# Storing part of the second two batches by column halves: attention with a soft mixture of experts on one core

## The chip, the core and the metric

The kernel runs on one core of a Trainium2 chip. The metric is the device time of the program in microseconds (us); lower is better. The kernel before has a median of 191.47 us over three runs (191.35 to 192.05). A core has five engines with a queue each: TensorE (PE; PEld is its weight load), VectorE (DVE), ScalarE (ACT), GpSimd (POOL) and SyncE (SP). Transfers between the chip's memory and a core's own memory run on 16 DMA engines.

## What is computed

```python
# q, k, v: [8 batches, 8 heads, 576 tokens, 64]
scores = scale * q @ k.T                  # window: each token sees itself and the 63 before
attn   = softmax(where(mask, scores, -1e9)) @ v
x      = attn.transpose(0, 2, 1, 3).reshape(4608, 512)

logits = x @ phi                          # [4608, 32]: 8 experts x 4 slots
d      = softmax(logits, over the tokens)
slot_input = (d.T @ x).reshape(8, 4, 512)
slot_out[e] = relu(slot_input[e] @ w1[e]) @ w2[e]      # w1: 512x1024, w2: 1024x512
c      = softmax(logits, over the slots)
out    = c @ slot_out                     # [4608, 512] float32
```

The softmax over the tokens needs all 4608 of them, so the experts start only when attention is done, and no row of the output can be written before the experts are done with at least the columns of that row that are written.

## The kernel before

The order of every instruction on every engine is written out by hand. The first 150 us (a loop over 32 pairs of heads) do attention, the logits and the slot inputs. What the change touches is the tail behind that, from the experts on.

**Experts.** `first` is the first layer (half of its columns at a time), `turn_hidden` transposes the hidden rows, `second` and `second_last` are the second layer. The second layer is made in two column halves of 256 (`d` = 0 and 1, `DH` = 256), each summed over all experts in its own PSUM tile `ops[d]`; `second_last(d)` does the last two experts, whose w2 weights arrive last (tile `w2h` for the last expert, loaded by GpSimd's queue, one half of the columns after the other). ScalarE then casts a half into `osb` (L904 and L910).

**Tokens.** The output is given out by pairs of batches, k = 0 to 3, of 1152 tokens each. A pair is laid out as 128 partitions of nine tokens (`NE` = 9, index e), so that the nine rows of a partition lie next to each other in the output. For a batch b, `ct_all[:, b]` holds the slot weights c before their division, in an order in which they can't be multiplied yet. `spread(b)` brings them in order: five products with 0/1 weights into the PSUM tile `rp`, then one copy into `ct4[b // 2]`, on ScalarE or VectorE (L662). `sums(k)` makes the nine row sums of a pair with nine one-column products into `rp` and takes their reciprocals on VectorE (L675, into `rcs`). There is one `rp` buffer: whoever writes it waits for whoever read it last.

**Giving out.** `give(k, e0, ne, c0, nc_)` makes tokens e0 to e0 + ne - 1 of all 128 partitions of pair k, columns c0 to c0 + nc_: one product for each token into a PSUM tile `cp` (four buffers, a bank each: two tokens of a column half, or one whole token), then for each token an eviction that multiplies by the reciprocal, on ScalarE (L899) or VectorE (L897) in turn, bank by bank (`turn`), into one of seven SBUF buffers, and a store from SyncE's queue (L901). A store of column halves writes pieces of 1 KB; one of whole rows writes ne rows that lie next to each other, 6 KB for three tokens. A store that reuses a buffer waits for the store seven before it.

The tail's order before: `second(0, .)`, `second_last(0)`, the first column half of pair 0 in stores of 2, 2 and 5 tokens, `second(1, .)`, `second_last(1)`, the second column half of pair 0 in stores of 4 and 5 tokens with `spread(2)` and `spread(3)` behind them, `sums(1)`, then pairs 1 to 3 as whole rows, three tokens at a time, with the spreads and sums of the next pair in between. That is 14 stores.

Of the kernel before, what the change touches and what calls it, by code (L numbers as in the profile page):

```python
# [9 lines left out]
FP32 = mybir.dt.float32  # L10
# [8 lines left out]
def kernel(  # L19
# [126 lines left out]
    DH = D // 2  # L146
# [11 lines left out]
    def w2_at(e, d, fc):  # L158
        return w2_t[e][d][fc] if e == last else w2_t[e][fc][:, DH * d:DH * d + DH]
# [331 lines left out]
    def cb_exp(b):  # L491
        ec = pw.tile([128, 6, 32], FP16, name="ec", tag="ec") if b < B - 1 else \
            lh[:, 6:8, :].rearrange("p i x -> p (i x)")[:, 0:192].rearrange("p (i s) -> p i s", s=32)
        nc.scalar.activation(ec[:, :, :], lgs.pop(b)[:, :, :], AF.Exp)
        cbs[b] = ec

    def cb_turn(b):
        nc.vector.transpose(ct_all[:, b, :], cbs.pop(b)[:, :, :].rearrange("p i s -> p (i s)"))
# [142 lines left out]
    NE = 2 * S // 128  # L641
# [12 lines left out]
    def spread(b, copy, rp=None):  # L654
        if rp is None:
            rp = psr.tile([128, 1024], FP32, name="rp", tag="rp")
        for t in range(5):
            w = 128 if t < 4 else 64
            nc.tensor.matmul(rp[:, 128 * t:128 * t + w], ss4[:, min(t, 3), :],
                             ct_all[:, b, 128 * (t // 4):128 * (t // 4) + w], start=True, stop=True,  # L660
                             skip_group_check=True)
        copy(out=ct4[b // 2][:, :, 64 * (b % 2):64 * (b % 2) + 64],  # L662
             in_=rp[:, 0:S].rearrange("p (x e) -> p e x", e=NE))
# [7 lines left out]
    def sums(k):  # L671
        rp = psr.tile([128, 1024], FP32, name="rp", tag="rp")
        for e in range(NE):
            nc.tensor.matmul(rp[:, e:e + 1], ct4[k][:, e, :], one[:, :], start=True, stop=True, skip_group_check=True)
        nc.vector.reciprocal(rcs[:, k, :], rp[:, 0:NE])  # L675

    b, p = B - 1, NP - 1
# [118 lines left out]
    psr = ctx.enter_context(tc.tile_pool(name="psr", bufs=1, space=bass.MemoryType.PSUM))  # L796
# [4 lines left out]
    def bank(name):  # L801
        t = psh.tile([128, 512], FP32, name=name, tag="ph")
        return t, t[:, :].bitcast(FP16)
# [23 lines left out]
    def turn_hidden(g):  # L827
        for i, copy in enumerate((nc.scalar.copy, nc.vector.tensor_copy)):
            _, th = bank("th")
            for c in range(4):  # L830
                nc.tensor.transpose(th[:, 128 * c:128 * c + 128], hs_[:, g, i, c, :], ident_h[:, :])
            copy(out=hT[g][:, 4 * i:4 * i + 4, :].rearrange("p c x -> p (c x)"), in_=th[:, 0:512])

    def second(d, g, js=range(4)):
        for fc in range(NFC):
            for j in js:
                nc.tensor.matmul(ops[d][32 * j:32 * j + 32, 0:DH], hT[g][:, fc, 32 * j:32 * j + 32],
                                 w2_at(4 * g + j, d, fc), start=(g == 0 and fc == 0), stop=False,
                                 skip_group_check=True)


    def second_last(d):
        for j in (2, 3):
            for fc in range(NFC):
                i = fc % 4
                nc.tensor.matmul(ops[d][32 * i:32 * i + 32, 0:DH], hT[1][:, fc, 32 * j:32 * j + 32],
                                 w2_at(4 + j, d, fc), start=False, stop=(j == 3 and fc >= 4), skip_group_check=True)

    act, dve = nc.scalar.copy, nc.vector.tensor_copy
# [15 lines left out]
    first(1, 1)  # L865
    second(0, 0)
    turn_hidden(1)
    cb_exp(b - 1)
    cb_turn(b - 2)
    second(0, 1, (0, 1))  # L870
# [9 lines left out]
    turn, piece = 0, 0  # L880

    def give(k, e0, ne, c0, nc_):
        nonlocal turn, piece
        ov = out[2 * S * k:2 * S * k + 2 * S, :].rearrange("(p e) d -> p e d", e=NE)
        ob = obs[piece % NRES][:, 0:ne * nc_].rearrange("p (e d) -> p e d", d=nc_)
        piece += 1
        n1 = 512 // nc_
        for i0 in range(0, ne, n1):
            n_ = min(n1, ne - i0)
            cp = pst.tile([128, n1, nc_], FP32, name="cp", tag="cp")  # L890
            for i in range(n_):
                nc.tensor.matmul(cp[:, i, :], ct4[k][:, e0 + i0 + i, :], osb[:, c0:c0 + nc_],  # L892
                                 start=True, stop=True, skip_group_check=True)
            for i in range(n_):
                rc = rcs[:, k, e0 + i0 + i:e0 + i0 + i + 1]
                if turn % 2:
                    nc.vector.tensor_scalar(out=ob[:, i0 + i, :], in0=cp[:, i, :], scalar1=rc, scalar2=None, op0=ALU.mult)  # L897
                else:
                    nc.scalar.activation(ob[:, i0 + i, :], cp[:, i, :], AF.Copy, scale=rc)  # L899
            turn += 1  # L900
        nc.sync.dma_start(out=ov[:, e0:e0 + ne, c0:c0 + nc_], in_=ob)  # L901

    second_last(0)
    act(out=osb[:, 0:DH], in_=ops[0][:, 0:DH])  # L904
    for e0, ne in ((0, 2), (2, 2), (4, 5)):
        give(0, e0, ne, 0, DH)
    second(1, 0)
    second(1, 1, (0, 1))
    second_last(1)
    act(out=osb[:, DH:D], in_=ops[1][:, 0:DH])  # L910
    for e0, ne in ((0, 4), (4, 5)):
        give(0, e0, ne, DH, DH)
        spread(2 + e0 // 4, (act, dve)[turn % 2])
    sums(1)
    for k in range(1, B // 2):
        for e0 in range(0, NE, 3):
            give(k, e0, 3, 0, D)
            if k < 3:
                if e0 < 6:
                    spread(2 * k + 2 + e0 // 3, (act, dve)[turn % 2])  # L920
                else:
                    sums(k + 1)
# [1 line left out]
_INS = ['q', 'k', 'v', 'moe_phi', 'moe_w1', 'moe_w2']  # L924
_OUTS = [((4608, 512), 'float32')]
# [25 lines left out]
```

## Time and profile before

| | |
|---|---|
| median of three runs | 191.47 us |
| the profiled execution | 191.22 us |
| its span, first to last instruction | 189.4 us |
| TensorE / VectorE / ScalarE busy | 160.4 / 142.9 / 144.9 us |
| stores of the output: issues, bytes | 14, 9.44 MB |
| first / last store issued | 160.49 / about 179.4 us |

The whole-kernel shares of busy time say little about the tail, the last 30 us. It is read by time windows (a row has the window, its length, then busy us and the number of instructions of TensorE, its weight loads, VectorE, ScalarE and GpSimd, then the granted TensorE clock, the mean busy share of the 16 DMA engines and the GB/s moved), by the timeline (start, us, engine, line, operation, and in brackets the idle time ahead of it and who ended it), and by the issues and landings of the stores. The share of the DMA engines can read somewhat over 1, since packets overlap.

### The profile page before, as it was taken

Reading aid. Unit: us, or ns where it says so; the run is one execution under the profiler, and the core shown is the slowest. Engines: PE = TensorE matmul, PEld = TensorE weight load, DVE = VectorE, ACT = ScalarE, POOL = GpSimd, SP = SyncE. Lnnn points to the kernel's source line nnn. Section 1 sums busy time; section 2 is a strip of 40 time slices with the busy share of each in tenths; the row PEclk is TensorE's granted clock in tenths of the full one; section 3 lists DMA queues with packets and bytes.
Section 4 is the critical chain, followed back from the end, with each engine's and each line's share of the span. In section 5 each row is a group of like instructions: output and inputs, shape, how many; then the busy total and the mean of one; then the engine's idle time right before and its main releaser. Section 6 shows DMA issues by size and latency. Waiting matters only on the chain. (4 is left out here: it accounts for less than half of the span.)

```text
span 189.4 us, 7060 instructions
## 1 busy us (share of the span) xinstructions
PE 160.4 (85%) x3036; PEld 120.5 (64%) x3036; DVE 142.9 (75%) x352; ACT 144.9 (76%) x266; POOL 98.5 (52%) x123
## 2 busy tenths in 40 slices
PE   5787999999999999999999899999989897769500
PEld 1466878877777777777777787776774365633100
DVE  6798796897888889788878988888886555289800
ACT  6487879989889898988999898988588256379600
POOL 7857927273695554983984828727854160000000
PEclk9999999999999999999999999999999999999955
DMA  6999999999999999999999999999999999979996
GB/s 153 222 184 185 226 175 223 179 223 179 185 226 180 210 192 184 207 196 185 210 195 192 211 182 198 199 204 195 213 214 212 204 196 179 277 258 422 415 415 252
DMA packets 61630, 41.47 MB, mean 219 GB/s; under 512 B 38816, under 2 KB 57504, under 8 KB 60704
## 3 DMA queue, kind: packets, MB, share of 16 engines
q0 software_dynamic: 56560, 30.35, 116.1%
q1 hardware_dynamic: 5040, 10.68, 15.9%
q8 instruction: 23, 0.38, 0.7%
q14 instruction: 7, 0.06, 0.1%
HBM read 61.93 MB, written 9.44 MB: 377 GB/s over the span
## 5 line engine op out<-in xcount | busy, mean ns | idle before, releaser
L336 ACT ACTIVATE qb<-a_q 64x576 f16<-64x576 f16 x63 | 40.6, 645 | 5.5 <-PE a_q L316 4.0
L353 DVE TENSOR_REDUCE m<-a_m 128x8 f16<-128x1024 f32 x32 | 39.2, 1224 | 1.0
L381 ACT ACTIVATE pt<-a_s 128x1024 f16<-128x1024 f32 x32 | 32.8, 1024 | 6.6 <-PE a_s L375 5.4
L180 POOL COPY v<-v 64x1152 f16<-64x1152 f16 x16 | 18.3, 1142 | 32.8 <-DMA v<-in_v_dram 32.6
L415 DVE TENSOR_TENSOR x_b<-a_v,rc 128x640 f16<-128x640 f32 x31 | 25.6, 825 | 1.1
L349 PEld LDWEIGHTS <-qb 128*128 128x128 f16 x256 | 16.8, 98 | 7.8 <-ACT qb L336 0.4
L346 PE MATMUL a_m<-wm,ident_h 128*128 128x512 f16 x64 | 19.3, 384 | 0.9 <-DVE m L353 0.9
L375 PEld LDWEIGHTS <-lh 128*128 128x128 f16 x288 | 18.8, 98 | 1.9 <-issue 1.7
L173 POOL DMA_DIRECT2D v<-in_v_dram x16 | 19.8, 1235 | 0.0
L372 PEld LDWEIGHTS <-kT 128*128 128x128 f16 x288 | 18.6, 98 | 1.6 <-issue 1.4
L372 PE MATMUL a_s<-qb,kT 128*128 128x128 f16 x256 | 19.5, 219 | 0.0
L349 PE MATMUL a_m<-kT,qb 128*128 128x128 f16 x256 | 19.5, 219 | 0.0
L375 PE MATMUL a_s<-rt,lh 128*128 128x128 f16 x256 | 19.5, 219 | 0.0
L433 ACT COPY xt<-a_k 128x576 f16<-128x576 f16 x28 | 17.9, 640 | 2.0 <-PE a_k L429 0.7
L182 POOL COPY v<-v 64x1088 f16<-64x1088 f16 (+1 forms) x16 | 17.9, 1120 | 0.8
L405 PE MATMUL a_v<-v,pt 128*64 128x65 f16 x558 | 15.6, 196 | 2.1 <-DVE m L363 1.1
L897 DVE TENSOR_SCALAR w<-cp,rcs 128x512 f32<-128x512 f32 (+1 forms) x22 | 12.9, 635 | 5.7 <-PE cp L892 5.4
L367 DVE CAST rt<-a_v 9x128 f16<-9x128 f32 x30 | 8.7, 289 | 11.0 <-PE a_v L366 10.7
L327 ACT ACTIVATE kT<-a_k 128x576 f16<-128x576 f16 x24 | 15.7, 654 | 0.8 <-PE a_k L316 0.8
L405 PEld LDWEIGHTS <-pt 128*64 128x64 f16 x576 | 13.5, 110 | 4.3 <-DVE m L363 1.8
L79 POOL DMA_DIRECT2D ks<-in_k_dram x15 | 10.4, 696 | 10.9 <-PE a_s L375 3.0
L316 PE MATMUL a_q<-ident_h,qs 96*64 96x96 f16 x384 | 14.7, 206 | 1.6 <-DVE a_q L225 1.3
(182 smaller groups left out, 332.6 us busy)
## 6 DMA issues: line engine op xcount, KB each, us to landing
w<-in_moe_w_dram POOLq DMA_DIRECT2D x13, 1024.0 KB, 16.8
out_dram<-w SPq DMA_DIRECT2D x9, 768.0 KB, 6.2
v<-in_v_dram POOLq DMA_DIRECT2D x16, 288.0 KB, 12.4
ks<-in_k_dram POOLq DMA_DIRECT2D x15, 288.0 KB, 15.2
qs<-in_q_dram POOLq DMA_DIRECT2D x15, 288.0 KB, 12.5
out_dram<-w SPq DMA_DIRECT2D x2, 640.0 KB, 4.4
w1h<-in_moe_w_dram POOLq DMA_DIRECT2D x4, 256.0 KB, 15.9
w<-in_moe_w_dram POOLq DMA_DIRECT2D x4, 256.0 KB, 14.8
```

The source lines that it names most:

```text
L173: nc.gpsimd.dma_start(out=v1s[b % 2][:, c, 0:Dh], in_=v[b].rearrange("h s d -> (h s) d").rearrange("(c p) d -> p c d", p=128)[:, c, :])
L180: nc.gpsimd.tensor_copy(out=v2[64:128, c0:c1, 0:Dh], in_=v1[0:64, c0:c1, 0:Dh])
L182: nc.gpsimd.tensor_copy(out=v2[0:64, c0:c1, 0:Dh], in_=v1[64:128, c0 - 1:c1 - 1, 0:Dh])
L336: nc.scalar.activation(qbs[p % NQ][h, :, hf, :], turned(a_qh)[h], AF.Copy, scale=QKS)
L346: nc.tensor.matmul(a_m[:, j, :], ident_h[:, :], wm[:, j:j + 4, :].rearrange("p c x -> p (c x)"), start=True, stop=False, skip_group_check= ...
L349: nc.tensor.matmul(a_m[:, i // 4, 128 * (i % 4):128 * (i % 4) + 128], qblock(p, i), kwindow(p, i), start=False, stop=True, skip_group_chec ...
L353: nc.vector.reduce_max(ms[p % 2][:, 64:72].rearrange("p (l c) -> p l c", l=2), a_m[:, :, :].rearrange("p l (c x) -> p l c x", x=128), axis ...
L372: nc.tensor.matmul(at(i), kwindow(p, i), qblock(p, i), start=(i % 4 == 0), stop=False, skip_group_check=True)
L375: nc.tensor.matmul(at(i), lh[:, i, :], rt[:, :], start=False, stop=True, skip_group_check=True)
L381: nc.scalar.activation(st_pt(p)[:, 0:8, :].rearrange("p i x -> p (i x)"), a_s[:, :, :], AF.Exp, scale=XS)
L405: nc.tensor.matmul(a_v[r0:r0 + 64, hf, 65 * (i // 2):65 * (i // 2) + 65], pt[:, i, 64 * hf:64 * hf + 64], rhs, start=True, stop=True, skip ...
L415: nc.vector.tensor_tensor(out=xbs[b][:, :, 128 * hp:128 * hp + 128].rearrange("p c (l d) -> p l c d", l=2), in0=avv[:, :, :, 0:64], in1=rc ...
```

## The change

`spread(2)` moves up to behind `turn_hidden(1)`. The products of `spread(3)` move ahead of the first `give` and its copy (VectorE) behind the second; for that `spread_product` makes the five products at once and keeps the copy for later in `late`. `sums(1)` moves ahead of `second_last(1)`. Three tokens of pair 1 are now stored by column halves: the first half ahead of `second_last(1)`, the second half behind pair 0's. The second column half of pair 0 is stored in pieces of 2, 3 and 4 tokens instead of 4 and 5. `spread(4)` and `spread(5)` come ahead of the whole rows of pair 1, `sums(2)` behind the first store of its whole rows, and pair 1 has two stores of whole rows instead of three. That is 16 stores.

```diff
     second(0, 0)
     turn_hidden(1)
+    spread(2, act)
     cb_exp(b - 1)
     cb_turn(b - 2)
     second(0, 1, (0, 1))
...
+    def spread_product(b):
+        rp = psr.tile([128, 1024], FP32, name="rp", tag="rp")
+        spread(b, lambda out, in_: late.append((out, in_)), rp)
+
     second_last(0)
     act(out=osb[:, 0:DH], in_=ops[0][:, 0:DH])
-    for e0, ne in ((0, 2), (2, 2), (4, 5)):
-        give(0, e0, ne, 0, DH)
+    late = []
+    spread_product(3)
+    give(0, 0, 2, 0, DH)
+    give(0, 2, 2, 0, DH)
+    dve(out=late[0][0], in_=late[0][1])
+    give(0, 4, 5, 0, DH)
     second(1, 0)
     second(1, 1, (0, 1))
+    sums(1)
+    give(1, 0, 3, 0, DH)
     second_last(1)
     act(out=osb[:, DH:D], in_=ops[1][:, 0:DH])
-    for e0, ne in ((0, 4), (4, 5)):
-        give(0, e0, ne, DH, DH)
-        spread(2 + e0 // 4, (act, dve)[turn % 2])
-    sums(1)
+    give(0, 0, 2, DH, DH)
+    give(0, 2, 3, DH, DH)
+    give(0, 5, 4, DH, DH)
+    spread(4, act)
+    give(1, 0, 3, DH, DH)
+    spread(5, dve)
     for k in range(1, B // 2):
-        for e0 in range(0, NE, 3):
+        for e0 in range(3 if k == 1 else 0, NE, 3):
             give(k, e0, 3, 0, D)
-            if k < 3:
+            if k == 1 and e0 == 3:
+                sums(2)
+            if k == 2:
                 if e0 < 6:
-                    spread(2 * k + 2 + e0 // 3, (act, dve)[turn % 2])
+                    spread(6 + e0 // 3, (act, dve)[turn % 2])
                 else:
-                    sums(k + 1)
+                    sums(3)
```

## The prediction

> **What bounds the kernel now.** First the chain that ended last, its last row and the span, and SyncE's own waits in the tail:
>
> ```profile
> span 189.4 us, 7060 instructions
> ...
> 178.82 0.58 ACTq L946
> ...
> SPq L946 <- DMA out_dram<-w: 7.5, 3, 3.8
> ```
>
> The chain stops at 179.4 us, 10 us before the span ends, and what waits at the end (L946) waits for stores to the output. So the end is set by how soon the output gets through the DMA engines, and an engine matters only as far as it lets a store leave late. Next the traffic: the page's rate in 40 slices, the time windows of one microsecond (last two columns: mean busy share of the 16 DMA engines, GB/s) where it is not full, and finer ones at the edges:
>
> ```profile
> GB/s 153 222 184 185 226 175 223 179 223 179 185 226 180 210 192 184 207 196 185 210 195 192 211 182 198 199 204 195 213 214 212 204 196 179 277 258 422 415 415 252
> ...
> 165.00:166.00 1.00, 0.94 (x11) 0.69 (x10) 1.00 (x3) 0.85 (x3) 0.00 (x0) 1.00 0.49 175
> 166.00:167.00 1.00, 0.54 (x6) 0.26 (x4) 1.00 (x3) 0.74 (x3) 0.00 (x0) 1.00 0.19 64
> 167.00:168.00 1.00, 0.34 (x10) 0.34 (x11) 0.65 (x2) 0.61 (x1) 0.00 (x0) 1.00 1.03 347
> 168.00:169.00 1.00, 1.00 (x11) 0.54 (x9) 0.69 (x2) 0.62 (x2) 0.00 (x0) 1.00 0.82 265
> ```
>
> ```profile
> 166.25:166.50 0.25, 0.00 (x0) 0.00 (x0) 0.25 (x2) 0.25 (x2) 0.00 (x0) 1.00 0.20 70
> 166.50:166.75 0.25, 0.23 (x5) 0.23 (x4) 0.25 (x1) 0.21 (x1) 0.00 (x0) 1.00 0.01 4
> 166.75:167.00 0.25, 0.18 (x4) 0.04 (x1) 0.25 (x2) 0.03 (x1) 0.00 (x0) 1.00 0.24 78
> ...
> 168.50:168.75 0.25, 0.25 (x5) 0.20 (x4) 0.22 (x1) 0.25 (x1) 0.00 (x0) 1.00 0.33 98
> ...
> 187.50:187.75 0.25, 0.00 (x0) 0.00 (x0) 0.00 (x0) 0.00 (x0) 0.00 (x0) 0.50 0.21 74
> ```
>
> By the last of these rows traffic ends at about 187.55 (0.21 of that quarter). The three full slices of the tail (422, 415, 415) give 417 GB/s for the whole-row pieces; a piece of column halves, whose pieces of a row are 1 KB, ran at 347 with the same full share. The hole is at 165 to 167: the share does not drop at once but falls to 0.49, then 0.20 and nothing by 166.5. Some of the 16 engines had finished the first three pieces, others had not. The stores' issue rows, each followed by the transfer row of the same window (last column: us from issue to landing), and the load that came last show why:
>
> ```profile
> 160.49 0.92 SPq L901 DMA_DIRECT2D out_dram<-w  x2
> out_dram<-w SPq DMA_DIRECT2D x2, 256.0 KB, 4.3
> 161.59 0.37 SPq L901 DMA_DIRECT2D out_dram<-w  x1
> out_dram<-w SPq DMA_DIRECT2D x1, 640.0 KB, 5.3
> 166.01 0.37 SPq L901 DMA_DIRECT2D out_dram<-w  x1
> out_dram<-w SPq DMA_DIRECT2D x1, 512.0 KB, 2.9
> 167.72 0.37 SPq L901 DMA_DIRECT2D out_dram<-w  x1
> out_dram<-w SPq DMA_DIRECT2D x1, 640.0 KB, 3.6
> 169.68 0.35 SPq L901 DMA_DIRECT2D out_dram<-w  x1
> out_dram<-w SPq DMA_DIRECT2D x1, 768.0 KB, 3.8
> ...
> 163.75 0.29 PE L846 MATMUL op<-w2h,hT 128*32 128x256 f16 x4 [0.78 <-DMA w2h<-in_moe_w_dram]
> ```
>
> The first 256 KB left at 160.49 and landed 4.3 later, at 164.8, one microsecond after the last weight load (163.75), though a lone 512 KB needs 2.9. I read this as: the engine that still had weights to load wrote nothing before, and its first store came behind its last load. It finished the three pieces at 166.5 (landing 161.59 + 5.3 = 166.9). Every store is split over all 16 engines, so a later store is done when the **latest engine** is. For that engine the tail is: idle 166.5 to about 166.95 (the next store left at 166.01 and needs some 0.95 to begin), 512 KB (524 kB / 347 = 1.51) to 168.45, idle to 168.7 (the next left at 167.72), 640 KB (1.89) to 170.6, then nine times 768 KB (786 kB / 417 = 1.886 each, 16.97) to 187.56. The trace says 187.55, so the model holds. It has about **0.7 us of idle** there; the mean over all engines shows far more.
>
> **The change, part by part.** Rows for what is added and moved (timeline; then groups by shape for 158.5 us to the end: count, busy us, mean ns):
>
> ```profile
> 157.18 0.83 PE L837 MATMUL op<-w,hT 128*32 128x256 f16 x12 [0.45 <-ACT hT L832]
> ...
> 158.74 0.37 ACT L904 CAST qb<-op 128x256 f16<-128x256 f32 x1 [1.10 <-PE op L846]
> 159.16 1.03 PE L892 MATMUL cp<-qb,v 128*128 128x256 f16 x8 [0.47 <-ACT qb L904]
> ...
> 159.80 1.66 DVE L897 TENSOR_SCALAR w<-cp,rcs 128x256 f32<-128x256 f32 x4 [1.74 <-PE cp L892]
> ...
> 162.16 0.29 PE L846 MATMUL op<-w,hT 128*32 128x256 f16 x2
> ...
> 164.93 0.88 DVE L897 TENSOR_SCALAR w<-cp,rcs 128x256 f32<-128x256 f32 x2 [3.47 <-PE cp L892]
> ...
> 165.15 1.57 ACT L899 ACTIVATE w<-cp,rcs 128x256 f32<-128x256 f32 x4 [0.69 <-PE cp L892]
> ...
> 166.52 0.41 PE L659 MATMUL rp<-ct_all,v 128*128 128x128 f16 x5 [0.40 <-DVE v L662]
> ...
> 171.15 0.38 PE L674 MATMUL rp<-one,v 128*128 128x1 f16 x9
> ```
>
> ```profile
> L899 ACT ACTIVATE w<-cp,rcs 128x512 f32<-128x512 f32 x14 | 8.6, 690 | 2.1 <-DVE rcs L675 2.1
> ...
> L899 ACT ACTIVATE w<-cp,rcs 128x256 f32<-128x256 f32 x9 | 3.5, 477 | 1.2 <-PE cp L892 1.2
> ...
> L662 DVE CAST v<-rp 128x576 f16<-128x576 f32 x3 | 2.2, 747 | 0.0
> ...
> L662 ACT CAST v<-rp 128x576 f16<-128x576 f32 x3 | 1.9, 638 | 0.5 <-PE rp L659 0.5
> ```
>
> - *spread(2)*, five products (0.41), goes where TensorE waits 0.45 for ScalarE's copy of hT: nothing. Its copy, 0.64 on ScalarE, pushes the two cb_exp and the cb_turn behind them back by 0.64; ScalarE had 1.10 free ahead of L904, so that cast still starts at 158.74. Without that cover it is 0.64 on the first pieces.
> - *spread(3)*, 0.41 on TensorE, fits the 0.47 in which it waits for that cast. Its copy, 0.75 on VectorE, stands ahead of the last two VectorE evictions of the third piece (they ended at 159.80 + 1.66 = 161.46), so that piece leaves at about 162.35 and not 161.59. It does not cost: the latest engine only begins storing after 163.5.
> - *sums(1) and the three half tokens of batches 2 and 3* (call this piece 4, 384 KB): 9 + 3 products, 0.38 and three eighths of 1.03, or 0.77 on TensorE ahead of second_last(1) (from 162.16), whose four last products wait 0.78 for the load. So 163.75 stays; if the load came 0.78 sooner, 0.77 would be on the second column half. VectorE: reciprocal, then two evictions (0.88), so it leaves at about 163.85.
> - *Second half.* Cast and first eviction stay (164.93). The first piece is two tokens, both VectorE's: 164.93 + 0.88, issue 165.87 instead of 166.01 (the old one waited a little for ScalarE too). Then ScalarE from 165.15 in twos (0.95 each, 2 x 477), with 0.64 for spread(4) and two 0.69 evictions: the pieces of three, four, three (batch 2 and 3) and the first whole one leave at about 166.35, 167.3, 168.7, 170.1; VectorE, with spread(5), sums(2) and its evictions, lets the next leave at 171.35.
> - *Stores*: 16, not 14: two more issues of 0.37 on SyncE, whose queue otherwise only waits in the tail: nothing. The last two reuse buffers of the eighth and ninth store, which by the sum below end at 172.2 and 174.1, long before the evictions get there: nothing. But 768 KB that went as one whole-row piece go as two half pieces: 786 kB at 347 instead of 417, 2.265 - 1.886 = **+0.38 us** for each engine.
>
> [...]
>
> *The sum for the latest engine*: 166.5, then without a gap 384, 256, 384, 512 and 384 KB (1.13, 0.755, 1.13, 1.51, 1.13; 5.66 together) to 172.16, and eight whole pieces (15.09) to 187.25, **0.3 us sooner**. It needs each store to leave 1 us before the one ahead of it ends: by 166.6, 167.4, 168.5, 170.0, 171.2 and 173.0 from the two-token piece on; the issues above are ahead of these by 0.7 to 1.7. The same from the differences: 0.7 of idle removed, 0.38 paid. Unknown is the rate of a late engine in half pieces when others idle or not. Bounds: 417 for all five (4.71, 0.95 less, so 1.25 sooner) and 0.7 idle paid back by a rate 6% under 347 (0.34 more, so nothing). I take 347, the row of the same kind of piece. Span 189.1; the profiled execution took 191.22 for 189.4, so 190.92, and the median shown is 0.25 above it: **191.2**.
>
> **Rivals.**
> 1. *The early engines set the end* (late ones catch up when the others are done). Idle share 0.51 + 0.81 + 0.18 at 165 to 169 is 1.5, less 0.38: 1.1 sooner, 190.4. For it: the hole is wide in the mean. Against: the stepwise fall of the share, and that full-share rates look set by the engine (347 with short rows at full share).
> 2. *The latest engine has no idle to give*: its stores already abut, only the +0.38 stays: 191.85. Against: 0.01 share at 166.5.
> 3. *The second column half comes late.* sums(1) waits for VectorE's late copy or its reciprocal, TensorE's second_last(1) with it, and the two-token piece leaves after 166.6: from there every delay is idle, and the change is slower from 166.9. With 0.7 of the TensorE work uncovered and the 0.75 copy in series, 1.45 late: 167.3, hence 0.7 - 0.3 = 0.4 above, 191.9; worse if the later pieces, on ScalarE without a gap, slip as well. Against: VectorE's copy ends at 161.4, TensorE gets there after 162.2.
> 4. *Every transfer has a fixed cost that is paid in series.* A lone 512 KB took 2.9, 1.39 over its 1.51; two more would cost 2.8: 194.2. Against: the full share through the last nine. [...]
>
> **How the numbers follow.** Forecast 0.60; rival 1 0.20; rival 2 0.08; rival 3 0.09; rival 4 0.03. About 0.5% (0.96 us) is what a measurement here can tell, so faster means under 190.5, slower over 192.4. Rival 1 is just past that line: 0.15 of it, with 0.03 of the forecast's own low end (down to 1.25 sooner), make 0.18 faster. Rival 4 and 0.07 of rival 3 make 0.10 slower; 0.72 remain. The range reaches to rival 1 and over rival 3: 190.2 to 192.1.
>
> **What would show it.** Right: the share at 165 to 169 stays above 0.6, with no quarter near 0.01; the share of the last microsecond falls stepwise instead of at once, since the early engines now end first; the two-token store leaves near 165.9; the wait for w2h shrinks to 0.1 or less and still ends near 163.75; the first whole piece leaves near 170.1. Wrong: traffic that ends at once near 186.4 (rival 1), a two-token store after 166.6 (rival 3), gaps in the share between stores that were issued in time (rival 4).

## The result, and the profile after

Over 22 runs each the changed kernel has a median of 191.25 us and the one before 191.75 us; the ratio is 0.9964, 95% interval 0.9949 to 0.9978. That is 0.7 us faster (0.4 to 1.0), where 0.3 was forecast. A ratio leaves out executions more than 1.5% above the fastest of the same kernel, here the changed kernel's two longest, with which the means are 0.5 us apart (191.29 and 191.83). The times lie between 189.82 and 192.79, those of before between 191.35 and 192.79: the best execution is 1.5 us under the best of before, the worst is the same.

The profiled execution of the changed kernel has the longer span. From its page, the span, the rate in 40 slices and the queue of kind instruction, whose packets are called fetches here (packets, MB, share of 16 engines' span):

```profile
span 190.5 us, 7073 instructions
...
GB/s 171 207 185 189 224 177 220 179 224 178 186 222 178 216 187 185 211 194 182 214 187 202 202 184 203 196 200 201 214 212 212 201 196 154 310 341 415 413 410 125
...
q8 instruction: 24, 0.39, 0.7%
```

Experts and stores lie 0.8 us later here than in the profile shown of before (the first store leaves at 161.27, not 160.49); what runs ahead of them is the same code in both. The rates of the two slices that were 277 and 258 are now 310 and 341. The same in time windows (last two columns: share of the DMA engines, GB/s):

```profile
164.00:165.00 1.00, 0.63 (x17) 0.49 (x17) 0.88 (x2) 0.80 (x2) 0.00 (x0) 1.00 1.03 347
165.00:166.00 1.00, 0.90 (x7) 0.68 (x7) 0.48 (x2) 0.32 (x2) 0.00 (x0) 1.00 0.98 329
166.00:167.00 1.00, 0.58 (x9) 0.53 (x8) 0.92 (x4) 1.00 (x4) 0.00 (x0) 1.00 1.04 359
167.00:168.00 1.00, 0.52 (x8) 0.32 (x6) 1.00 (x3) 1.00 (x3) 0.00 (x0) 1.00 0.94 311
168.00:169.00 1.00, 0.95 (x8) 0.33 (x6) 0.80 (x2) 1.00 (x3) 0.00 (x0) 1.00 1.04 343
```

The hole is gone. The end of the traffic before, in quarters of a microsecond, and then after the change:

```profile
187.25:187.50 0.25, 0.00 (x0) 0.00 (x0) 0.00 (x0) 0.00 (x0) 0.00 (x0) 0.50 1.19 492
...
187.75:188.00 0.25, 0.00 (x0) 0.00 (x0) 0.00 (x0) 0.00 (x0) 0.00 (x0) 0.50 0.01 0
```

```profile
186.75:187.00 0.25, 0.00 (x0) 0.00 (x0) 0.00 (x0) 0.00 (x0) 0.00 (x0) 0.50 0.95 393
187.00:187.25 0.25, 0.00 (x0) 0.00 (x0) 0.00 (x0) 0.00 (x0) 0.00 (x0) 0.50 0.50 197
187.25:187.50 0.25, 0.00 (x0) 0.00 (x0) 0.00 (x0) 0.00 (x0) 0.00 (x0) 0.50 0.07 25
...
188.75:189.00 0.25, 0.00 (x0) 0.00 (x0) 0.00 (x0) 0.00 (x0) 0.00 (x0) 0.50 0.06 25
```

From 187.25 to 189.0 the share is 0.06 or 0.07, about one sixteenth: fifteen engines are done and a single one works on. The trace has 16 reports of each store's landing, which I take for one from each of the 16 engines: 15 report the last store between 187.45 and 187.75, one at 189.44. It was within 0.3 of the others up to the store that landed at 180.2 and 2 us behind from the next on. Between these two landings lies the 24th packet of the instruction queue: 16 KB, 0.93 us, starting at 182.15. The kernel before has 23, the last of them at 162.84. The row of that queue in the changed kernel's window from 182 to 183.2 us, and the one in the page of before:

```profile
q8 instruction: 1, 0.02, 4.8%
...
q8 instruction: 23, 0.38, 0.7%
```

Two theories came out of this. **A**, the prediction's: the latest engine sets the end, 0.7 of idle against 0.38 paid. **C**, its first rival with an addition: late engines catch up, so about 1.1 us are gained, and the extra fetch takes it back where it falls among the stores. (In the first expectations it is called B and has no cause yet for the one engine's delay.)

### The profile page after: what moved, and what is told of

The parts are those of the page before. It is cut to its first block, busy times and chain, and to the rows that moved or that the text cites. A ratio compares the mean times of both kernels' runs of the same rounds, so it can differ in the third digit from the quotient of the medians.

```text
span 190.5 us, 7073 instructions
## 1 busy us (share of the span) xinstructions
PE 162.3 (85%) x3039; PEld 121.6 (64%) x3039; DVE 142.7 (75%) x354; ACT 145.1 (76%) x267; POOL 98.8 (52%) x123
## 4 chain that ended last, share of the span: by engine, by line
PE 44%; DVE 26%; issue 7%; ACT 7%; DMA 4%; POOL 4%; DVEq 0%; ACTq 0%; POOLq 0%
DVE m L353 7%; PE a_m L346 5%; PE a_m L349 5%; DVE x_b L415 4%; PE a_q L316 4%; PE a_s L372 3%; PE a_v L405 3%; PE a_s L375 3%; DMA out_dram<-w 3%; PE a_k L316 2%; DVE acc L526 2%; DVE kT L324 2%; PE a_k L429 2%; PE ha L816 2%; DVE rt L367 2%
## 5 line engine op out<-in xcount | busy, mean ns | idle before, releaser
L349 PEld LDWEIGHTS <-qb 128*128 128x128 f16 x256 | 17.3, 99 | 8.5 <-ACT qb L336 0.8
L349 PE MATMUL a_m<-kT,qb 128*128 128x128 f16 x256 | 20.0, 222 | 0.3 <-ACT qb L336 0.3
L346 PE MATMUL a_m<-wm,ident_h 128*128 128x512 f16 x64 | 19.8, 391 | 0.2 <-DVE m L353 0.2
L316 PE MATMUL a_q<-ident_h,qs 96*64 96x96 f16 x384 | 15.2, 211 | 1.2 <-DVE a_q L225 1.0
L898 DVE TENSOR_SCALAR w<-cp,rcs 128x256 f32<-128x256 f32 (+1 forms) x24 | 13.5, 611 | 2.1 <-PE cp L893 1.7
```

The lines of the kernel that those rows point to most:

```text
L316: nc.tensor.transpose(tq[64 * hf:64 * hf + 64, RP * r:RP * r + RP], src[0:RP, h + hf, Dh * r:Dh * r + Dh], ident_h[0:RP, 0:RP])
L346: nc.tensor.matmul(a_m[:, j, :], ident_h[:, :], wm[:, j:j + 4, :].rearrange("p c x -> p (c x)"), start=True, stop=False, skip_group_check= ...
L349: nc.tensor.matmul(a_m[:, i // 4, 128 * (i % 4):128 * (i % 4) + 128], qblock(p, i), kwindow(p, i), start=False, stop=True, skip_group_chec ...
```

## The experiments

**The changed kernel a second time.**

> The changed kernel once more, for a second profile. In the first one 15 of the 16 DMA engines landed the last store at 187.45 to 187.75 us and one engine at 189.44; it fell 2 us behind between two stores near 181. Theory A (the latest engine of all 16 sets the end, with a steady lag from the loads; 0.7 us idle removed, 0.38 paid): the same lag of one engine shows again, time 0.3 us under before. Theory B (the late engines catch up, about 1.1 us are gained, and in some executions one engine loses up to 2 us by itself): either no engine lags and the span is about 1.1 under that of before, or one lags at another place and the gain is gone; times spread over more than 2 us.

Ratio 0.9973 (0.9943 to 1.0002), times from 190.28 to 192.16. The page again, and the end of the traffic:

```profile
q8 instruction: 24, 0.39, 0.8%
```

```profile
187.00:187.25 0.25, 0.00 (x0) 0.00 (x0) 0.00 (x0) 0.00 (x0) 0.00 (x0) 0.50 0.32 123
...
187.75:188.00 0.25, 0.00 (x0) 0.00 (x0) 0.00 (x0) 0.00 (x0) 0.00 (x0) 0.50 0.06 25
...
188.50:188.75 0.25, 0.00 (x0) 0.00 (x0) 0.00 (x0) 0.00 (x0) 0.00 (x0) 0.50 0.06 25
```

One engine is last again, but it is no lag from the loads: it sets in between the landings at 178.9 and 182.0, and the 24th fetch is at 178.33 this time. The packets around it that took over 0.3 us (0.33, 0.46 and 0.46 ahead, the fetch's 0.92, 0.64 behind, against 0.24 for a usual 6 KB packet) add up to 1.85 us over the usual, about what the engine lost (1.9 to 2.1 in the landings). They are the only long ones after 174 us. The first profile has five such packets too, from 180.6 to 183.7, the fetch among them, and no other. The trace does not name a packet's engine; I take them for that engine's. A falls as to the end, B gets its addition.

**Three tokens by column halves alone.** In the kernel before, at the old place:

```diff
-            give(k, e0, 3, 0, D)
+            if k == 1 and e0 == 0:
+                give(k, e0, 3, 0, DH)
+                give(k, e0, 3, DH, DH)
+            else:
+                give(k, e0, 3, 0, D)
```

> The kernel before, with the first three tokens of batches 2 and 3 stored as two stores of column halves instead of one of whole rows, at their old place; nothing else moves. Measures the term of 0.38 us by itself. Theories A and B: 0.3 to 0.4 slower (1 KB pieces at 347 GB/s against 417). [...] If the first half leaves sooner than the whole rows did, up to 0.3 of it comes back.

Ratio 1.0043 (1.0016 to 1.0070), 0.3 to 1.3 us slower. Its time windows:

```profile
172.00:173.00 1.00, 0.84 (x7) 0.23 (x4) 0.77 (x2) 1.00 (x3) 0.00 (x0) 1.00 1.04 342
173.00:174.00 1.00, 0.95 (x12) 0.53 (x13) 1.00 (x2) 0.47 (x1) 0.00 (x0) 1.00 1.03 347
174.00:175.00 1.00, 0.63 (x7) 0.35 (x6) 0.91 (x3) 0.49 (x1) 0.00 (x0) 1.00 1.10 440
175.00:176.00 1.00, 0.71 (x4) 0.20 (x3) 1.00 (x3) 1.00 (x3) 0.00 (x0) 1.00 0.98 393
```

Full share all through, 342 to 347 GB/s in half pieces and over 390 in whole rows. From the last w2h product to the last landing it takes 24.85 us, before 24.46: 0.39 more. So in the stretch that it was made for the term of 0.38 holds, in one profile. The whole time rose by more, 0.8, and what the rest is, is not shown: this kernel has three products more as well, like the changed one (below), and its profile no 24th fetch.

**The second half in pieces of 4 and 5 again**, the rest as changed:

```diff
-    give(0, 0, 2, DH, DH)
-    give(0, 2, 3, DH, DH)
-    give(0, 5, 4, DH, DH)
+    give(0, 0, 4, DH, DH)
+    give(0, 4, 5, DH, DH)
```

> The changed kernel with the second column half of batches 0 and 1 in pieces of 4 and 5 tokens again; all else stays. Both theories: the early half store of batches 2 and 3 covers the wait for the four-token piece, so the time stays that of the changed kernel within 0.2 us. If the two-token piece carries the gain, 0.3 or more slower than the changed kernel.

Ratio 0.9973 (0.9943 to 1.0004), like the changed kernel beside it. The two-token piece gives nothing that can be measured.

**The changed kernel without the early half store**, batches 2 and 3 all as whole rows:

```diff
     sums(1)
-    give(1, 0, 3, 0, DH)
     second_last(1)
...
     spread(4, act)
-    give(1, 0, 3, DH, DH)
     spread(5, dve)
     for k in range(1, B // 2):
-        for e0 in range(3 if k == 1 else 0, NE, 3):
+        for e0 in range(0, NE, 3):
```

> The changed kernel without the early half store: all tokens of batches 2 and 3 leave as whole rows behind the second column half, the spreads and sums stay moved. Theory A: idle of the latest engine 0.35 of the 0.7 stays, the 0.38 are not paid, so 0.3 to 0.4 under before, like the changed kernel. Theory B: the early engines stay idle from 165.1 to 166.9 again, only the second hole closes, 0.2 to 0.4 under before and some 0.7 over the changed kernel.

Ratio 0.9993 (0.9970 to 1.0016). From the last w2h product to the last landing 24.19, 0.27 under before, where the changed kernel's 15 undelayed engines have 23.40. These are B's numbers: of the 1.06 us by which the stretch got shorter, 0.79 are the early half store's. The times of the two kernels alone do not tell (their intervals overlap).

**Fewer TensorE instructions.** The change adds three products, each with its weight load, so TensorE has six instructions more. The pages before and after:

```profile
PE 160.4 (85%) x3036; PEld 120.5 (64%) x3036; DVE 142.9 (75%) x352; ACT 144.9 (76%) x266; POOL 98.5 (52%) x123
...
PE 162.3 (85%) x3039; PEld 121.6 (64%) x3039; DVE 142.7 (75%) x354; ACT 145.1 (76%) x267; POOL 98.8 (52%) x123
```

That is 6072 and 6078 in all; the expectations below count four fewer for both, 6068 and 6074. Here the changed kernel leaves out three of its ten `fill` products, which compute nothing:

```diff
-    fill(3, a_k[:, :])
+    fill(2, a_k[:, :])
...
-    fill(5, a_k[:, :])
+    fill(4, a_k[:, :])
...
-    fill(2, a_k[:, :])
+    fill(1, a_k[:, :])
```

> The changed kernel with three of its ten idle-time products (fill) left out, one at each place, so that TensorE has 6068 instructions like the kernel before and not 6074; nothing else moves. In both profiles of the changed kernel one more 16 KB instruction fetch than before (24 instead of 23) falls among the last stores, and the DMA engine that carries it ends 1.2 to 1.7 us after the others. Theory C (the late engines catch up, 1.1 us are gained, and the fetch takes it back where it falls among the stores): 23 fetches, all engines end within 0.5 us, 0.8 to 1.2 us under before, and no executions 1.5 us over the best. Theory A (0.3 us from the latest engine, the fetch a chance companion): still 0.3 under before.

Ratio 0.9958 (0.9938 to 0.9979), 0.8 us under before; times from 190.13 to 191.49. The page, and the end of the traffic:

```profile
q8 instruction: 23, 0.38, 0.7%
```

```profile
187.50:187.75 0.25, 0.00 (x0) 0.00 (x0) 0.00 (x0) 0.00 (x0) 0.00 (x0) 0.50 1.01 418
187.75:188.00 0.25, 0.00 (x0) 0.00 (x0) 0.00 (x0) 0.00 (x0) 0.00 (x0) 0.50 0.15 49
188.00:188.25 0.25, 0.00 (x0) 0.00 (x0) 0.00 (x0) 0.00 (x0) 0.00 (x0) 0.50 0.00 0
```

All engines end together, with 23 fetches.

**More TensorE instructions in the kernel before**: one `fill` product more at each of the same places, so as many as after the change.

> The kernel before with three more idle-time products, so that TensorE has 6074 instructions; the stores stay as they were. Theory C: a 24th fetch; where it falls among the stores one engine ends 1.2 to 1.9 us late, in about half of the executions, so 0.4 to 0.9 us slower in the mean, with a wider spread. Theory A and any theory by which the fetch costs nothing: within 0.2 us of before (the added products lie where TensorE waits).

Ratio 1.0008 (0.9984 to 1.0032) without its two longest runs, 193.85 and 194.53: a miss for C's size. With them the mean of its twelve runs is 192.26 against 191.73 for before, 0.5 more and inside what C forecast. Two runs decide between the two, and the profile has 23 fetches and all engines together at the end, so by itself this is inconclusive.

**Two early half tokens**, the other seven of batches 2 and 3 as 3, 2 and 2 whole rows, with the three `fill` products left out:

```diff
-    give(1, 0, 3, 0, DH)
+    give(1, 0, 2, 0, DH)
...
-    give(1, 0, 3, DH, DH)
+    give(1, 0, 2, DH, DH)
...
-        for e0 in range(3 if k == 1 else 0, NE, 3):
-            give(k, e0, 3, 0, D)
-            if k == 1 and e0 == 3:
+        for e0, ne in ((2, 3), (5, 2), (7, 2)) if k == 1 else ((0, 3), (3, 3), (6, 3)):
+            give(k, e0, ne, 0, D)
+            if k == 1 and e0 == 5:
```

> As the first, but only two tokens of batches 2 and 3 by column halves, the other seven as whole rows in threes and twos. A third of the 0.38 us for 1 KB pieces is not paid (0.13), and the early half store of 256 KB still covers the wait for the two-token piece to within 0.1 to 0.4 us. All theories: within 0.2 of the first; 0.1 faster if the cover is enough, 0.2 slower if the early engines set the end.

Ratio 0.9967 (0.9942 to 0.9992): no difference from three tokens that these runs tell.

**The kernel before a second time.**

> The kernel before once more, for a second profile: 23 fetches, all engines within 0.3 us at the end, traffic all but nothing for half a microsecond or more ahead of the first store of the second column half.

As expected; its windows at the hole:

```profile
165.50:166.00 0.50, 0.44 (x5) 0.24 (x4) 0.50 (x3) 0.50 (x3) 0.00 (x0) 1.00 0.55 191
166.00:166.50 0.50, 0.24 (x1) 0.07 (x1) 0.50 (x2) 0.50 (x3) 0.00 (x0) 1.00 0.21 72
166.50:167.00 0.50, 0.37 (x5) 0.26 (x4) 0.50 (x3) 0.33 (x1) 0.00 (x0) 1.00 0.06 20
```

**Without and with the three `fill` products, on one chip.** First without:

> The changed kernel with 6068 TensorE instructions again, on the same chip as the changed kernel itself. Theory C (fetch among the stores costs one DMA engine some 1.9 us in those executions where it falls there): 0.3 to 0.7 under the changed kernel in the mean, and no execution in the band 1.5 us over the best. Rival (the fetch costs nothing on the whole, one engine catches up or ends late by chance): the two within 0.2 us and spread alike.

Ratio 0.9931 (0.9906 to 0.9956) over six runs, from 190.20 to 190.91. And with them:

> The changed kernel again beside the first. Theory C: some executions as fast as the best of the first kernel, the others 1 to 2 us over. The profile: a 24th fetch of 16 KB behind the last product, and if it falls before 187 us one engine ends 1.2 us or more after the others.

Ratio 0.9975 (0.9949 to 1.0001), times from 189.87 to 192.18. The intervals just overlap; the means are 190.52 and 191.25. The profile of this one has no 24th fetch, and there it ends as the lean one does:

```profile
187.00:187.25 0.25, 0.00 (x0) 0.00 (x0) 0.00 (x0) 0.00 (x0) 0.00 (x0) 0.50 0.95 393
187.25:187.50 0.25, 0.00 (x0) 0.00 (x0) 0.00 (x0) 0.00 (x0) 0.00 (x0) 0.50 0.21 74
187.50:187.75 0.25, 0.00 (x0) 0.00 (x0) 0.00 (x0) 0.00 (x0) 0.00 (x0) 0.50 0.00 0
```

So the same code gave a last landing at 189.4 with the fetch among the stores and at 187.9 without it, both with the first store at 161.3. Over all runs of the three series of the changed kernel 19 of 46 runs took more than 191.49 us, the most that any of the 18 lean runs took; the means are 191.24 and 190.71.

**TensorE work ahead of second_last(1) alone**, in the kernel before, with three other `fill` products left out as above (an excerpt of the edit):

```diff
     second(1, 1, (0, 1))
+    fill(3, psr.tile([128, 1024], FP32, name="rp", tag="rp")[:, 0:512])
     second_last(1)
```

> The kernel before with three dummy products, some 0.7 us of TensorE, ahead of second_last(1), where the change put 0.77; three idle-time products are left out elsewhere, so TensorE has 6068 instructions. If the wait for the last weights covers it (the prediction): the time of before within 0.1. If that wait is often shorter, as the profiles with 4.41 us from the first output product to the last w2h product and no wait say (against 3.64 with neither): 0.1 to 0.4 slower than before.

Ratio 1.0008 (0.9985 to 1.0031): 0.15 us slower, between -0.3 and 0.6, which tells neither. In its profile no wait for w2h is left, and the way from the first output product to the last w2h product is 4.51 us.

**Pieces of 4 and 5 without the three `fill` products.**

> The first kernel with the second column half of batches 0 and 1 in pieces of 4 and 5 instead of 2, 3 and 4; one store less. All theories: within 0.2 us of the first. From the last w2h product to the last landing 23.4 to 23.7 us as there; 24.0 or more if the two-token piece matters.

Ratio 0.9956 (0.9933 to 0.9980), and 23.61 us after the last w2h product: the two-token piece does not matter here either.

What the profiles have in common, in us, from the trace (last column: the last landing after the start of the last w2h product):

| kernel | first output product to last w2h product | first store to last landing | last w2h product to last landing |
|---|---|---|---|
| before; again | 4.60; 4.03 | 27.7; 27.2 | 24.46; 24.47 |
| before, more TensorE instructions | 4.44 | 27.6 | 24.46 |
| before, filled | 4.51 | 27.6 | 24.44 |
| before, half rows | 3.64 | 27.2 | 24.85 |
| no early half store | 4.30 | 27.2 | 24.19 |
| changed, fetch among the stores (two profiles) | 4.41; 4.43 | 28.2; 28.1 | 25.09; 24.99 |
| the same, its 15 other engines | | 26.5; 26.9 | 23.40; 23.75 |
| changed, no such fetch | 4.61 | 26.6 | 23.34 |
| changed, lean (three `fill` products fewer; two profiles) | 4.41; 4.60 | 26.5; 26.8 | 23.44; 23.57 |
| pieces of 4 and 5; the same, lean | 4.41; 4.41 | 26.7; 26.7 | 23.60; 23.61 |
| two early half tokens, lean | 4.61 | 26.9 | 23.61 |

## Why the prediction was right, and what in it was not

*What bounds the tail.* Right: the stores' traffic, and the holes in it. With the holes closed, the stretch behind the last w2h product is about 1.0 us shorter wherever no fetch intrudes (24.46 to between 23.3 and 23.6).

*The sum for the latest engine.* This is the term that was mis-sized most: five half pieces at 347 GB/s, 5.66 us, from the third store on. The landings of the third store in the changed kernel's first profile reach from 166.11 to 167.48, those of the eighth only from 172.25 to 172.58. Between the last landings lie 5.10 us for what was put at 5.66 (385 GB/s if all engines did so), inside the bounds given but 0.56 from the value taken; between the first landings lie 6.14, and the mean share fell to 0.69 in the quarter of a microsecond from 165.75 and to 0.79 and 0.85 in the two from 167.0: I read this as the early engines waiting a little for two of the stores. So the lag shrank from 1.37 to 0.33 us before the whole rows began, by this reading about half of it by the early engines' waits (0.48 over the 5.66) and half by a late engine faster than 347 (0.56 under it). In the five profiles with these same stores, lean ones included, the last landings lie 5.10 to 5.52 apart, always under 5.66. Most of the mean idle became gain: rival 1's mechanism, nearly with its 1.1. The prediction's own signs say the same. In the changed kernel's profile without a 24th fetch the traffic ends at once, not stepwise, at about 187.5, with the first store 0.8 later than before; rival 1, shifted by as much, has 187.2 and the forecast 188.0. Why a late engine is faster in these pieces no run here tells apart.

*The price of 1 KB pieces.* Right in the stretch of the stores: +0.39 measured alone in one profile, +0.38 forecast.

*spread(2) and spread(3).* Right, as the rows of the changed kernel show: the products stand in what was idle, and TensorE's wait for hT is 0.20 instead of 0.45.

```profile
157.35 0.42 PE L659 MATMUL rp<-ct_all,v 128*128 128x128 f16 x5
...
157.97 0.83 PE L837 MATMUL op<-w,hT 128*32 128x256 f16 x12 [0.20 <-ACT hT L832]
...
159.39 0.43 PE L659 MATMUL rp<-ct_all,v 128*128 128x128 f16 x5
...
159.94 1.03 PE L893 MATMUL cp<-qb,v 128*128 128x256 f16 x8
```

From the first op product to the first output product it is 4.02 us, and 4.04 before.

*sums(1) and the early half products are covered by the wait for the last weights.* Only in part. In the changed kernel no wait is left:

```profile
163.35 0.38 PE L674 MATMUL rp<-one,v 128*128 128x1 f16 x9
163.59 0.49 PE L893 MATMUL cp<-qb,v 128*128 128x256 f16 x3
164.01 0.40 PE L846 MATMUL op<-w,hT 128*32 128x256 f16 x8
164.24 0.39 PE L846 MATMUL op<-w2h,hT 128*32 128x256 f16 x8
```

The way to the last w2h product is 4.41, against 3.64 in the one profile of the old order that does not wait either: the 0.77 that the prediction priced, for the case that the load comes sooner, and put at nothing in its sum. The old order's other profiles have 4.60, 4.03 and 4.44 with their waits, so what comes uncovered is between nothing and 0.77, depending on how the loads stand to TensorE in that execution; its mean could not be measured alone.

*The second half's issues.* Right in that all were in time: with the 0.8 us by which everything is later, forecast 166.65 for the two-token piece and 169.5 for the last half piece; they left at 166.42 and 168.60, the latter 0.9 sooner than forecast:

```profile
166.42 0.37 SPq L902 DMA_DIRECT2D out_dram<-w  x1
```

```profile
168.60 0.37 SPq L902 DMA_DIRECT2D out_dram<-w  x1
```

Nothing came late (rival 3), the idle was there (rival 2 falls), and two more transfers did not add a fixed cost (rival 4 falls: the stretch got shorter with 16 stores than with 14). Before the change, the last landings of the nine whole-row stores are 1.76 to 1.91 us apart, and 786 kB at the measured 417 GB/s take 1.886.

*What was missing.* The extra fetch. The gain of 1.0 in the stores, less what TensorE's 0.77 costs uncovered, less about 1.2 to 1.7 us in the executions where the fetch falls among the stores, leaves the 0.7 measured. That the forecast of 0.3 was near is therefore partly chance: a gain taken too small, one cost put at nothing and one not seen. The forecast of 191.2 beside the measured 191.25 is luck once more: the kernel before came out at 191.75 in these runs, 0.28 over the median that the forecast started from. That three products decide the fetch is suggested by counts, not shown: with 6072 TensorE instructions or fewer none of eight profiles has it, with 6078 three of six have it (in the kernel with pieces of 4 and 5 it came at 190.14, behind the stores and the span, so its page counts 23). All three are of the changed order of the tail; the two kernels of the old order with 6078 have none. What exactly sets it off stays open. That it costs half a microsecond in the mean rests on the lean kernel's two series; in the kernel before, three products more did not show it clearly, and the kernel before with three fewer was not run, so what leaving them out gives by itself is not known.

The changed kernel without three `fill` products is the best version tried: 0.9958 and 0.9931 against before. The granted clock was 0.956 in one of its two profiles and 0.965 in that of the variant with 4 and 5, against 0.974 to 0.984 in all others. In the trace of the first (rows of one microsecond, the clock third from the end) it stands at 0.55 and 0.50 in two rows around the start of the experts:

```profile
149.00:150.00 1.00, 1.00 (x5) 0.28 (x2) 0.93 (x4) 0.19 (x1) 0.00 (x0) 0.55 1.16 200
150.00:151.00 1.00, 1.00 (x7) 0.25 (x5) 0.97 (x4) 0.58 (x2) 0.26 (x1) 0.50 1.27 203
```

But that does not show a price of the products left out. A mean clock of 0.965 or less came in 8 of the 39 runs of the versions with three fewer, in 10 of the 46 of the changed kernel with all ten, and in none of 90 runs of the kernel before. So it goes with the changed kernel, not with the products left out; the cause is open. Fewer instructions at another place were not tried.

## What to carry to other kernels

Where transfers set the end, fill the queue before the producers pause, even at the price of less efficient pieces: 0.4 us paid here for 1.4 us of hole closed. Don't carry one DMA engine's lag forward as if it stayed (here it shrank from 1.37 to 0.33 us over five stores); look at how each store's landings spread, store by store. And a few more instructions may bring one more instruction fetch (here in three of six profiles with 6078 TensorE instructions, in none of eight with 6072 or fewer): compare the count of instruction fetches between two pages before a tail of a microsecond is put down to anything else.

## What the runs showed of the hardware that was not expected

A fetch of instructions is one packet: all 24 in the changed kernel's first trace have 16 KB, and the one among the stores took 0.93 us. In the two profiles that have it there, one DMA engine's landings fell about 2 us behind, and the packets next to it took 0.33 to 0.64 us instead of 0.24; that they are that engine's, and that the fetch delayed it, is my reading, since the trace names no packet's engine. The 24th fetch came at 178, 182 or 190 us, 1 to 12 us after TensorE's last product, or not at all. And each store's landing has 16 reports in the trace, as many as there are DMA engines; one late report put the end 1.69 us behind the other 15 (189.44 against 187.75), with a share of 0.06 for over 1.5 us.
